# Zero rows of a padded weight by DMA, and up to two repeats of a score pass, in a fused attention and MLP kernel

## The chip, the cores and the metric

The kernel runs on one core of one Trainium2 chip. The metric is the device time of one execution in microseconds (us); lower is better. A kernel's time is the median of several executions. A profile is one further execution, recorded by the hardware profiler: its span is the time from the first to the last instruction.

## The reference

The sequence has S = 2048 rows of D = 640 bf16 values; attention has H = 32 heads of Dh = 20; the MLP has 1536 hidden columns. All of it is computed from one input x:

```python
g = sigmoid((x * gate_w).sum(-1, keepdims=True))
q, k, v = split(x @ wqkv)                    # 32 heads of 20
a = softmax(q @ k.T * Dh**-0.5) @ v          # per head, over all 2048 keys
a = concat_heads(a) @ wo
h = x @ w1 + b1
b = (h * tanh(softplus(h))) @ w2
out = g * a + (1 - g) * b
```

## The kernel before

**Units and slots.** Heads are taken in NG = 8 groups of HG = 4, queries in NC = 4 chunks of 512, keys in 16 tiles of 128. One unit is (c, g, kt, j): the scores of 512 queries of chunk c against 128 keys, for head j of group g. There are 2048 units, packed three to a slot, so 683 slots. A slot fills three PSUM banks, and there are two such sets of banks (banks 0 to 2 and 3 to 5). TensorE writes the three score tiles of a slot as one pass (L778: three matmuls of 32 rows that stand in different rows of the array). ScalarE takes the exponential of all three banks in one instruction (L806, 128x1536) and writes bf16 to one of five ETS buffers. TensorE multiplies these with v (L903, four heads at a time, in bank ACC = 6). Column 0 of v is one, so the sums of the softmax come out as a row of the same product.

**Units on VectorE.** In some slots the third unit is computed on VectorE instead, by bit arithmetic and a polynomial: L820 reads the bank, then L838, L840, three L843 and one L844 give the exponential in an OFF buffer. The exponential on ScalarE is then 128x1024. `choose` decides this from how far VectorE is behind in the plan.

**Background work.** Bank FB = 7 is shared by all else that TensorE does: projections to Q and K (L447, evicted by VectorE at L464) and V (L479, L487), the MLP's first product (L595, L605), its second (L659, evicted at L666), and the product with wo (L683, evicted and mixed at L689). Only one task holds the bank at a time, and the next must wait for the eviction. The mish function of the MLP is on ScalarE (L625) and VectorE (L645 to L652).

**The plan.** The order of instructions on every engine is written out ahead of time by a Python planner. `pl.now[engine]` is the planner's own clock of each engine, and each operation has a fixed cost. Per step the planner emits the exponential of slot `step` (`emit_e`), the scores of slot `step + 2` (`emit_s`), perhaps a repeat of that score pass (`repeat_s`, L790), the start of a VectorE unit (`emit_x`), at most two passes of products with v (`emit_pv`), and background matmuls. Engines run their instructions strictly in this order. So a matmul that waits holds all later matmuls.

A repeat writes the same scores into the same banks again. It is put where TensorE's planned stream of work would otherwise be less than STREAM = 0.46 of ScalarE's planned time; `to_come` counts the products and background work that the same step is expected to add. The exponential waits for the last repeat.

**End of a group of heads.** When the 16 key tiles of a (c, g) are through, `emit_off` must first have brought in all units of that group that VectorE computes; until then `emit_pv` returns without a product ("stuck"). Then VectorE copies bank ACC to OUNG (L967), SP sends the four rows of sums to RR (L970), VectorE inverts them (L974), SP writes them to SUMS in DRAM (L975) and spreads them to BCT (L977), and VectorE multiplies (L946) into OTN, or into QT for chunks 2 and 3.

**The padded output weight.** A head's 21 rows (sum and 20 values) stand at partitions 32j to 32j + 20, so wo is laid out in WOQ with the same gaps: rows 32j + 1 to 32j + 20 hold wo, the other 48 rows must be zero. WOQ holds the padded query weights first. When the last Q projection is issued, `load_wo` puts one memset of all of WOQ (128x5120) on GpSimd (L578) and four DMAs of wo on SP (L581), which wait for the memset. GpSimd also copies the padded weights of Q and K (L436).

Of the kernel before, what the change touches and what calls it, by code (L numbers as in the profile page):

```python
# [9 lines left out]
BF16 = mybir.dt.bfloat16  # L10
# [6 lines left out]
P = 128  # L17
S = 2048
D = 640
NF = 1536  # L20
H = 32
DH = 20
NG = 8
HG = 4
# [21 lines left out]
HOP = 0.1  # L46
TAIL = {"pe": 0.17, "act": 0.12, "dve": 0.125, "pool": 0.1, "sp": 2.0}
SWITCH = 0.1
COL = 1 / 2400.0
PASS = CW * COL  # L50
EXP = 1.335
STREAM = 0.46
EXP_PAIR = 0.908
# [124 lines left out]
def bass_gated_mix__softmax_full_mha__dense_activation_mish__prompt_kernel(  # L178
# [30 lines left out]
    WOQ = sb("WOQ", [P, NG * D], BF16)  # L209
# [4 lines left out]
    OTN = sb("OTN", [P, 2, NG, CW], BF16)  # L214
# [18 lines left out]
    FLAG = sb("FLAG", [1, 1], I32)  # L233

    SUMS = nc.dram_tensor("SUMS", [HG, CW], FP32, kind="Internal")

    def xt(c):
        return XB[:, c, :].rearrange("p (f t) -> p f t", t=CW)
# [38 lines left out]
    WOG = WOQ[:, :].rearrange("p (g c) -> p g c", c=D)  # L277
# [11 lines left out]
    off = {}  # L289
    off_units = {}  # L290

    def attention(pl, fast):
# [7 lines left out]
        soon = [deque() for _ in range(LANES)]  # L300
        norm = deque()
        acts = deque()
        now = {"step": -1, "open": None, "bank": False, "rate": 9.0}


        if fast:
# [7 lines left out]
        low_last = [None]  # L314
# [62 lines left out]
        wkv_read, wq_read = [], []  # L377
# [5 lines left out]
        wog_ready = []  # L383
# [5 lines left out]
        if fast:  # L389
# [17 lines left out]
            m_padq = pl.add("dve", lambda e: e.memset(PADQ, 0.0), cost=0.4)  # L407
            m_padk = pl.add("dve", lambda e: e.memset(PADK, 0.0), cost=0.4)
            m_acc = pl.add("dve", lambda e: e.memset(PS[:, ACC, :], 1.0), cost=0.5)
            m_one = pl.add("pool", lambda e: e.memset(V_all[:, :, :, 0:1], 1.0), cost=2.4)  # L410

            warm = None
            for i in range(20):
# [8 lines left out]
                B1T[:, :], B_b1.rearrange("(f p) -> p f", p=P), allow_slow_non_contiguous=True), (), "b1")  # L422
            g_load = pl.add("pool", lambda e: e.dma_start(
                GW[:, :], gate_w.rearrange("(f p) -> p f", p=P), allow_slow_non_contiguous=True), (), "gw")
            gw_col = pl.add("pool", lambda e: e.tensor_copy(WV[:, :, D], GW[:, :]), [g_load])
            pad_done, pad_read = {}, {}

# [147 lines left out]

            def load_wo():
                assert len(sq_ops) >= 4
                z = pl.add("pool", lambda e: e.memset(WOQ[:, :], 0.0), list(wq_read), cost=4.7)  # L578
                wo_v = A_wo.rearrange("(g j r) c -> j r g c", g=NG, j=HG, r=DH)
                for j in range(HG):  # L580
                    wog_ready.append(pl.add("sp", lambda e, j=j: e.dma_start(  # L581
                        WOG[32 * j + 1:32 * j + 1 + DH, :, :], wo_v[j]), [z], f"wo{j}", cost=0.6))

            h_done, b_read = {}, {}
            u_free, w_free = [None, None], [None]
# [116 lines left out]
        def p_task(c, t, half, due):  # L702

            tb = c * 4 + t

            def ready():
                if any((c, g) not in otn_done for g in every) or (fast and (tb, half) not in bdone):
                    return None
                if fast and len(wog_ready) < HG:
                    return None  # L710
                return [otn_done[(c, g)] for g in every] + wog_ready

            def finish(bank, last):
                otn_read[c % 2].append(last)
                ev = mix(OUTT[:, of(half)], bank, tb, ball(tb)[:, of(half)],
                         [last, bdone.get((tb, half)), *out_dma.values()])
                if half == 1:
                    store(tb, OUTT[:, :], [ev])
                return ev

            return Task([p_mm(c, t, half, g, every) for g in every], HALF * COL, finish, due, ready)
# [36 lines left out]
        queue = deque()  # L758
        hold = {"until": 0}
# [27 lines left out]
        def repeat_s(s):  # L787

            for i, (c, g, kt, j) in enumerate(slots[s]):
                s_op[s] = pl.add("pe", lambda e, i=i, c=c, g=g, kt=kt, j=j: e.matmul(  # L790
                    scores(s)[:, i, :], KT[32 * j:32 * j + 32, g, kt * P:(kt + 1) * P],
                    QT[32 * j:32 * j + 32, g, c * CW:(c + 1) * CW], start=True, stop=True,
                    tile_position=(32 * j, 0)), [], cost=PASS if i == 0 else 0.004, kind="S")
# [113 lines left out]

        def emit_pv(step, passes):

            while passes and step >= hold["until"]:  # L910
                if not queue:
                    return
                c, g, kt, _ = queue[0][2]
                emit_off((c, g), False)
                n = HG - sum(u[2] == kt for u in off_units.get((c, g), ()) if fast)
                if len(queue) < n:
                    return
                if kt == NKT - 1 and not emit_off((c, g), True):
                    if step < NSLOT - 1:
                        return  # L920
                    flush(lambda: emit_off((c, g), True, True))
                passes -= 1
                for k in range(n):
                    s, i, (c, g, kt, j) = queue.popleft()
                    op = pv_slot[s] = pv(c, g, kt, j, ETS[:, s % NETS, i, :], [e_op[s]], k == 0)
                    pv_left[s] -= 1
                if kt == NKT - 1:
                    hold["until"] = step + PV_HOLD
                    group_done(c, g, step, op)
# [4 lines left out]
        def group_done(c, g, step, last):  # L934


            end = c == NC - 1 and g == NG - 1

            def reads():
                if fast:  # L940
                    return [low_last[0]] if c >= 2 else []
                assert c < 2 or g > 0 or len(otn_read[c % 2]) == 8
                return otn_read[c % 2]

            def times(src, deps):
                oung_free[0] = bc_read[0] = otn_done[(c, g)] = pl.add("dve", lambda e: e.tensor_tensor(  # L946
                    otn(c, g, fast), src, BC, ALU.mult), [*deps, *reads()], cost=WIDE)
                if g == NG - 1:
                    otn_read[c % 2] = []

            if end:
                while norm:
                    norm.popleft()[1]()
                flush(lambda: not any(soon))
                src = PS[:, ACC, :]
                a = pl.add("dve", lambda e: e.transpose(BC, src), [last, bc_read[0]], cost=0.7)
                a = pl.add("dve", lambda e: e.reciprocal(RR[:, :], BC[:, 0:CW:32]), [a, rr_read[0]], cost=0.25)
                a = pl.add("dve", lambda e: e.transpose(
                    BC.rearrange("p (a r) -> p a r", r=32), RR[:, :].unsqueeze(2).to_broadcast([P, 16, 32])),
                    [a], cost=0.7)  # L960
                times(src, [a])
                acc_free[0] = oung_free[0]
                return
            while oung_free[0] == "busy":
                norm.popleft()[1]()
            src = OUNG[:, :]
            ev = dve(lambda e: e.tensor_copy(src, PS[:, ACC, :]), [last, oung_free[0]], WIDE)  # L967
            oung_free[0] = "busy"
            acc_free[0] = ev
            got = pl.add("sp", lambda e: e.dma_start(  # L970
                RR[:, :], OUNG[0:P:32, :].rearrange("j (r a) -> j r a", a=16)), [ev, rr_read[0]], "nr0", cost=0.55, tail=1.4)

            def invert():
                r = pl.add("dve", lambda e: e.reciprocal(RR[:, :], RR[:, :]), [got], cost=0.25)  # L974
                rr_read[0] = pl.add("sp", lambda e: e.dma_start(  # L975
                    SUMS.ap().rearrange("j (r a) -> (j r) a", a=16), RR[:, :]), [r, *spread_last], "nr1", cost=0.4, tail=1.7)
                spread_last[:] = [pl.add("sp", lambda e: e.dma_start(  # L977
                    BC, SUMS.ap().unsqueeze(1).to_broadcast([HG, 32, CW])),
                    [rr_read[0], bc_read[0]], "nr2", cost=0.55, tail=4.7)]
                spread = list(spread_last)  # L980
                norm.append((WIDE, lambda: times(src, spread), lambda: spread[-1]))
            norm.append((0.25, invert, lambda: got))
# [126 lines left out]
        for step in range(NSLOT + 40):  # L1109
# [28 lines left out]
            if step + 2 < NSLOT:  # L1138
                compose(step + 2, choose(step + 2) if fast and (step < slot_of(0, 1, 0) or behind < CATCH_UP) else None)
                emit_s(step + 2)  # L1140

                to_come = 0.0 if step < hold["until"] else min(2, len(queue) // HG) * PASS
                if owed + rate > 0.1 and pick(pl.now["pe"] + 0.8):
                    to_come += min(owed + rate, 0.4)
                if share[-1][0] + PASS + to_come < STREAM * (share[-1][2] + (EXP_PAIR if fast and step + 1 in off else EXP)):
                    repeat_s(step + 2)
                if fast and step + 2 in off:
                    emit_x(step + 2)
            emit_pv(step, 2 if step < NSLOT - 1 else 99)
# [15 lines left out]
        c = NC - 1  # L1165
# [151 lines left out]
```

## Time and profile before

| | |
|---|---|
| Three runs | 924.34, 927.46, 927.84 us (median 927.46) |
| Profiled execution | 926.2 us, of which the span is 924.3 us |
| TensorE clock granted, mean | 0.982 of full speed |
| Busy: ScalarE, VectorE, TensorE (matmul) | 895.4, 840.5, 771.0 us |
| GpSimd | 18.5 us in 25 instructions |
| Exponentials L806 | 683, of them 122 two banks wide |
| VectorE units (L820) | 58 + 63 = 121 |
| Score matmuls L778, repeated ones L790 | 2048, 465 |

How to read the lines below: PE is TensorE (PEld its weight loads), ACT ScalarE, DVE VectorE, POOL GpSimd, SP the engine that issues most DMAs. A line of the timeline has the start and the length in us, the engine, the source line, the operation with output and input tiles, the count, and in brackets how long the engine had stood idle and what released it. The page cuts the span into 40 slices of 23.1 us; its digits are tenths.

### The profile page before, as it was taken

The numbers are of one execution on the slowest core, as the hardware profiler recorded it, in microseconds if no ns is written. First come the engines' busy times: TensorE is split into PE (matmuls) and PEld (weight loads), VectorE is DVE, ScalarE is ACT, GpSimd is POOL, SyncE is SP. The second block draws the span as 40 slices with busy tenths as digits, with TensorE's granted clock in tenths as the row PEclk, the third lists the DMA queues.
The fourth block names the chain that finished last, engine by engine and source line by source line (L and its number), as shares of the span: only waits on it lengthen the run. The fifth ranks groups of instructions, "written<-read, shape, count | busy, mean of one in ns | idle before, by whom it ended". The sixth has DMA issues, their size and how long they took to land.

```text
span 924.3 us, 16089 instructions
## 1 busy us (share of the span) xinstructions
PE 771.0 (83%) x6649; PEld 262.2 (28%) x6701; DVE 840.5 (91%) x1561; ACT 895.4 (97%) x738; POOL 18.5 (2%) x25
## 2 busy tenths in 40 slices
PE   7788888887888888787998888889878888887986
PEld 2223222222323323232233222223223332232232
DVE  2498998789999999998999999999999999999874
ACT  5999999999999999998999999999999999999995
POOL 1000000000000000001000000000000000000000
PEclk9999999999999999998999999999999999999598
DMA  9001000000010100004111111111111211110001
GB/s 221 1 14 41 13 14 13 2 27 27 28 41 28 29 27 28 13 14 139 24 39 38 56 54 39 51 38 49 48 38 41 62 48 42 48 51 14 13 13 33
DMA packets 63136, 35.97 MB, mean 39 GB/s; under 512 B 22224, under 2 KB 59088, under 8 KB 63056
## 3 DMA queue, kind: packets, MB, share of 16 engines
q1 hardware_dynamic: 59040, 32.40, 13.1%
q10 hardware_dynamic: 3936, 2.46, 0.9%
q8 instruction: 55, 0.90, 0.4%
q14 instruction: 25, 0.20, 0.1%
q0 software_dynamic: 80, 0.00, 0.0%
HBM read 29.10 MB, written 2.88 MB: 35 GB/s over the span
## 4 chain that ended last, share of the span: by engine, by line
ACT 91%; PE 4%; DVE 3%; DMA 1%; issue 0%
ACT ETS L806 89%; PE PS L778 1%; ACT U L625 1%; ACT REG L625 1%; DMA XB<-in_A_x_dram 1%; PE PS L903 1%; PE PS L659 1%; DVE OFF L840 1%; PE PS L447 0%; PE PS L790 0%; ACT W2R L625 0%; DVE W2R L843 0%; DVE ETS L689 0%; DVE REG L820 0%; PE PS L479 0%
## 5 line engine op out<-in xcount | busy, mean ns | idle before, releaser
L806 ACT ACTIVATE ETS<-PS 128x1536 bf16<-128x1536 f32 (+1 forms) x683 | 884.2, 1578 | 8.9 <-PE PS L778 7.2
L778 PE MATMUL PS<-QT,KT 32*128 32x512 bf16 x2048 | 272.9, 390 | 127.0 <-ACT ETS L806 115.9
L903 PE MATMUL PS<-ETS,V_all 128*21 128x512 bf16 x1927 | 212.3, 391 | 0.2
L778 PEld LDWEIGHTS PS<-QT,KT 32*128 32x128 bf16 x2048 | 67.2, 91 | 350.0 <-ACT ETS L806 330.5
L648 DVE RECIPROCAL T<-T 128x256 f32<-128x256 f32 x48 | 83.4, 1738 | 0.0
L903 PEld LDWEIGHTS PS<-ETS,V_all 128*21 128x21 bf16 x1927 | 48.5, 89 | 119.7 <-issue 111.1
L659 PE MATMUL PS<-W2R,HB 128*128 128x320 bf16 x384 | 73.6, 311 | 4.1 <-DVE QT L464 3.4
L790 PE MATMUL PS<-QT,KT 32*128 32x512 bf16 x465 | 62.7, 391 | 0.0
L595 PE MATMUL PS<-XB,REG 128*128 128x256 bf16 x360 | 53.2, 275 | 0.0
L820 DVE TENSOR_SCALAR W2R<-PS 128x512 int32<-128x512 f32 x58 | 39.4, 686 | 13.1 <-PE PS L778 12.0
L820 DVE TENSOR_SCALAR REG<-PS 128x512 int32<-128x512 f32 x63 | 42.9, 682 | 5.4 <-PE PS L778 2.9
L447 PE MATMUL PS<-XB,WOQ 128*128 128x512 bf16 x135 | 40.2, 383 | 5.9 <-issue 2.4
L447 PE MATMUL PS<-XB,REG 128*128 128x512 bf16 x133 | 40.9, 384 | 3.9 <-issue 2.4
L843 DVE SCALAR_TENSOR_TENSOR REG<-REG,EM 128x512 f32<-128x512 f32 x64 | 43.5, 679 | 0.1
L844 DVE SCALAR_TENSOR_TENSOR OFF<-REG,OFF 128x512 bf16<-128x512 f32 x63 | 42.8, 681 | 0.1
L843 DVE SCALAR_TENSOR_TENSOR REG<-REG,ER 128x512 f32<-128x512 f32 x62 | 42.0, 678 | 0.2
L659 PEld LDWEIGHTS PS<-W2R,HB 128*128 128x128 bf16 x384 | 30.5, 99 | 39.9 <-issue 24.9
L843 DVE SCALAR_TENSOR_TENSOR W2R<-W2R,EM 128x512 f32<-128x512 f32 x58 | 39.5, 681 | 0.2
L843 DVE SCALAR_TENSOR_TENSOR W2R<-W2R,ER 128x512 f32<-128x512 f32 x58 | 39.4, 679 | 0.1
L844 DVE SCALAR_TENSOR_TENSOR OFF<-W2R,OFF 128x512 bf16<-128x512 f32 x58 | 39.0, 678 | 0.2
L595 PEld LDWEIGHTS PS<-XB,REG 128*128 128x128 bf16 x360 | 29.3, 98 | 22.1 <-issue 19.7
L479 PE MATMUL PS<-REG,XB 128*128 128x80 bf16 (+1 forms) x640 | 33.0, 201 | 2.1 <-DVE MXS L544 1.5
(101 smaller groups left out, 813.4 us busy)
## 6 DMA issues: line engine op xcount, KB each, us to landing
REG<-in_B_w_dram SPq DMA_DIRECT2D x36, 320.0 KB, 3.2
BCT<-SUMS SPq DMA_DIRECT2D x31, 256.0 KB
W2R<-in_B_w_dram SPq DMA_DIRECT2D x12, 320.0 KB, 3.2
W2R<-in_B_w_dram SPq DMA_DIRECT2D x1, 1920.0 KB, 8.0
out_dram<-OUTT SPq DMA_DIRECT2D x12, 160.0 KB, 1.8
REG<-in_A_wqkv_dram ACTq DMA_DIRECT2D x2, 700.0 KB, 5.9
WOQ<-in_A_wo_dram SPq DMA_DIRECT2D x4, 200.0 KB
WOQ<-in_A_wqkv_dram ACTq DMA_DIRECT2D x1, 700.0 KB, 8.6
```

Of the source, the lines that this page charges most:

```text
L447: return lambda e, bank: e.matmul(PS[:, bank, :], pads[:, b, f, :], xt(c)[:, f, :], start=(f == 0), stop=(f == NFT - 1))
L479: return lambda e, bank: e.matmul(PS[:, bank, t * n:(t + 1) * n], xt(c)[:, f, t * P:(t + 1) * P], WV[:, f, g * HD:g * HD + n], start=(f == ...
L595: return lambda e, bank: e.matmul(PS[:, bank, i * HW:(i + 1) * HW], w1b(n1)[:, f, i * P:(i + 1) * P], xt(c)[:, f, cols], start=(f == 0), s ...
L648: piece(RECIP, lambda e: e.reciprocal(T1[:, :], T1[:, :]))
L659: return lambda e, bank: e.matmul(PS[:, bank, 0:HALF], HB[:, hc % 2, f, t * P:(t + 1) * P], W2[:, f, half * HALF:(half + 1) * HALF], start ...
L778: last = pl.add("pe", lambda e, i=i, c=c, g=g, kt=kt, j=j: e.matmul(scores(s)[:, i, :], KT[32 * j:32 * j + 32, g, kt * P:(kt + 1) * P], QT ...
L790: s_op[s] = pl.add("pe", lambda e, i=i, c=c, g=g, kt=kt, j=j: e.matmul(scores(s)[:, i, :], KT[32 * j:32 * j + 32, g, kt * P:(kt + 1) * P], ...
L806: e_op[s] = pl.add("act", lambda e: e.activation(ETS[:, s % NETS, 0:n, :], scores(s)[:, 0:n, :], AF.Exp, scale=SCALE), [s_op[s], pv_slot.g ...
L820: ev_op[s] = dve(lambda e: e.tensor_scalar(x, scores(s)[:, 2, :], SCALE * LOG2E, BIAS, ALU.mult, ALU.add), [s_op[s], ei_free[b], *(wkv_rea ...
L843: piece(WIDE, lambda e, i=i: e.scalar_tensor_tensor(r, r if i else m, POLY[i], m, ALU.add, ALU.mult))
L844: piece(WIDE, lambda e: e.scalar_tensor_tensor(to, r, POLY[3], to, ALU.add, ALU.mult))
L903: return pl.add("pe", lambda e: e.matmul(PS[32 * j:32 * j + EW, ACC, :], V_all[:, kt, h, :], src, start=(count == 0), stop=(count == NKT - ...
```

## The change

1. `load_wo` no longer puts a memset on GpSimd. The four wo DMAs wait directly for the readers of the old contents. Five more DMAs on SP write the zero rows: one for partitions 0, 32, 64 and 96, and one for each of the four gaps of eleven rows. Their source is a new DRAM row ZEROS, read once for each destination row.
2. ZEROS is filled at the start: VectorE zeroes a corner of OTN (8 x 640), and a DMA on GpSimd's queue, put ahead of the copy `gw_col`, sends it to DRAM. The first products into OTN depend on that DMA.
3. A product with WOQ is ready when any entry is in `wog_ready` (there are now nine, all put in at once), and depends on all of them.
4. `emit_pv` records in `now["stuck"]` that products were held up by VectorE units. The next step then counts no products in `to_come`.
5. Up to two repeats of a score pass per step instead of one. The second must fit under the same target with its own length added. Each repeat must also end, by the planner's clock, before the running exponential does.

```diff
+    ZEROS = nc.dram_tensor("ZEROS", [1, NG * D], BF16, kind="Internal")
...
+            blank = OTN[0:NG, 0, 0:2, :].rearrange("p g t -> p (g t)")[:, 0:D]
+            m_blank = pl.add("dve", lambda e: e.memset(blank, 0.0), cost=0.25)
...
+            zeros = pl.add("pool", lambda e: e.dma_start(
+                ZEROS.ap().rearrange("o (g c) -> (o g) c", c=D), blank), [m_blank], "zero")
             gw_col = pl.add("pool", lambda e: e.tensor_copy(WV[:, :, D], GW[:, :]), [g_load])
...
             def load_wo():
-                z = pl.add("pool", lambda e: e.memset(WOQ[:, :], 0.0), list(wq_read), cost=4.7)
                 wo_v = A_wo.rearrange("(g j r) c -> j r g c", g=NG, j=HG, r=DH)
                 for j in range(HG):
                     wog_ready.append(pl.add("sp", lambda e, j=j: e.dma_start(
-                        WOG[32 * j + 1:32 * j + 1 + DH, :, :], wo_v[j]), [z], f"wo{j}", cost=0.6))
+                        WOG[32 * j + 1:32 * j + 1 + DH, :, :], wo_v[j]), list(wq_read), f"wo{j}", cost=0.6))
+                for n, rows in enumerate([slice(0, P, 32)] + [slice(32 * j + 1 + DH, 32 * j + 32) for j in range(HG)]):
+                    dst = WOQ[rows, :]
+                    wog_ready.append(pl.add("sp", lambda e, dst=dst: e.dma_start(
+                        dst, ZEROS.ap().to_broadcast([dst.shape[0], NG * D])), [*wq_read, zeros], f"wz{n}", cost=0.6))
...
-                if fast and len(wog_ready) < HG:
+                if fast and not wog_ready:
                     return None
...
         def emit_pv(step, passes):
+            now["stuck"] = False
...
                     if step < NSLOT - 1:
+                        now["stuck"] = True
                         return
...
-                    return [low_last[0]] if c >= 2 else []
+                    return [low_last[0]] if c >= 2 else [zeros]
...
-                to_come = 0.0 if step < hold["until"] else min(2, len(queue) // HG) * PASS
+                to_come = 0.0 if step < hold["until"] or now["stuck"] else min(2, len(queue) // HG) * PASS
...
-                if share[-1][0] + PASS + to_come < STREAM * (share[-1][2] + (EXP_PAIR if fast and step + 1 in off else EXP)):
-                    repeat_s(step + 2)
+                next_exp = EXP_PAIR if fast and step + 1 in off else EXP
+                want = STREAM * (share[-1][2] + next_exp)
+                for n in range(1, 3):
+                    if (share[-1][0] + n * PASS + to_come < want
+                            and pl.now["pe"] + PASS + TAIL["pe"] + 2 * HOP <= pl.now["act"] + next_exp):
+                        repeat_s(step + 2)
```

More of the change, by code (lines that the diff above doesn't have):

```diff
@@ L302, in attention @@
         acts = deque()
-        now = {"step": -1, "open": None, "bank": False, "rate": 9.0}
+        now = {"step": -1, "open": None, "bank": False, "rate": 9.0, "stuck": False}
         if fast:
```

## The prediction

> **What bounds the kernel now.** I read the page first (busy shares, then the slices), then the stretches view around the slices where ScalarE or the TensorE clock dips, then the timeline there, the chain of waits for the pace, and the view of waits.
>
> ```profile
> PE 771.0 (83%) x6649; PEld 262.2 (28%) x6701; DVE 840.5 (91%) x1561; ACT 895.4 (97%) x738; POOL 18.5 (2%) x25
> ...
> ACT  5999999999999999998999999999999999999995
> ...
> PEclk9999999999999999998999999999999999999598
> ...
> ACT ETS L806 89%; PE PS L778 1%; ACT U L625 1%; ACT REG L625 1%; DMA XB<-in_A_x_dram 1%; PE PS L903 1%; PE PS L659 1%; DVE OFF L840 1%; PE PS L447 0%; PE PS L790 0%; ACT W2R L625 0%; DVE W2R L843 0%; DVE ETS L689 0%; DVE REG L820 0%; PE PS L479 0%
> ```
>
> ScalarE is the bound: 97% busy, and its exponentials (L806) are 89% of the chain. So a change can only gain where ScalarE idles or is given less work. ScalarE has one dip inside the span (19th slice), and the clock has two (19th and 38th).
>
> ```profile
> 429.00:442.00 13.00, 9.10 (x56) 2.54 (x55) 11.69 (x17) 8.35 (x7) 4.36 (x1) 0.74 0.33 66
> 853.00:876.00 23.00, 22.36 (x142) 4.42 (x138) 19.30 (x35) 21.48 (x17) 0.00 (x0) 0.55 0.05 14
> 442.00:853.00 411.00, 349.53 (x2979) 123.39 (x2975) 406.71 (x743) 411.00 (x346) 0.00 (x0) 1.00 0.15 43
> ```
>
> In these stretches (columns: length, then busy time of PE, PEld, DVE, ACT, POOL, then clock and DMA) ScalarE is without a gap from 442 to 853, loses 4.65 us in the first dip and 1.52 us in the second. The first dip, in the timeline:
>
> ```profile
> 429.75 4.36 POOL L578 MEMSET WOQ<- 128x5120 bf16 x1 [96.46 <-PE PS L447]
> 430.19 4.21 DVE L840 TENSOR_SCALAR OFF<-REG 128x512 uint16<-128x512 uint16 x1
> 434.14 1.52 SPq L581 DMA_DIRECT2D WOQ<-in_A_wo_dram  x4
> 434.31 0.67 DVE L464 CAST QT<-PS 128x512 bf16<-128x512 f32 x1
> 435.13 1.23 PE L659 MATMUL PS<-W2R,HB 128*128 128x320 bf16 x4 [3.35 <-DVE QT L464]
> 436.95 1.45 ACT L806 ACTIVATE ETS<-PS 128x1536 bf16<-128x1536 f32 x1 [3.25 <-PE PS L778]
> 439.20 1.45 ACT L806 ACTIVATE ETS<-PS 128x1536 bf16<-128x1536 f32 x1 [0.80 <-PE PS L778]
> ```
>
> An L840 that elsewhere takes 0.42 us took 4.21 us, and ended just after the GpSimd memset did. Behind it on VectorE stood the eviction L464 of bank FB; TensorE, in order, stood 3.35 us at the matmul L659 that needs that bank, with the next scores behind it; ScalarE ran dry for 3.25 us. TensorE then had half its clock (0.50 in the stretches from 435 to 440), which gave the 0.80 and, at 441.25, another 0.59.
>
> **Part 1, the memset goes.** The pace of ScalarE comes from the chain: six wide exponentials in a row took 8.06 us, so 1.343 each; a run of six with one two-bank exponential took 7.63, so 0.915 for that one. In the dip the run before ended at 433.70, of which 0.11 is the tail of a lone one (1.45 against 1.343), and two wide ones lie between there and 441.25: 441.25 - 433.59 - 2 x 1.343 = 4.97 us lost. Without the memset L840 takes 0.42, L464 starts near 430.6 and TensorE does not stop; next late is nothing before ScalarE itself. Gain 5.0; bounds 3.25 (if the clock falls anyway) to 5.0.
>
> **Part 2, the zeros by DMA.** The memset of 8 x 640 on VectorE: 0.59 us at most (the row of L407, 128 x 640), in the 2.52 us for which VectorE waits for its first weights. The DMA that fills ZEROS on GpSimd's queue: 0.87 to 1.17 us (rows of L421, L423) inside GpSimd's 6.19 us wait for GW. The first OTN product waits for ZEROS too; it runs at 55.3 us and the nearest DMAs there took 7.0 us: nothing. On SP four loads of wo now issue at about 430.25 instead of 434.14, and five zero DMAs behind them: 1.52 + 5 x 0.38 = 3.4 us, so SP is free at 433.7; the next on SP, SUMS<-RR, went at 436.98. Their 480 KB take 2.0 us at the rate of W2R (1920 KB in 8.0) or 3.7 at the rate of wo here (130 GB/s); WOQ is first read by L683 at 489.9. Behind them in the queue stand SUMS and BCT of one normalisation; before, SUMS took 5.6 us to land behind the wo loads and VectorE waited for a BCT only once, 0.6 us. The test for readiness (any load in wog_ready, not four) and the nine loads that a product with WOQ names instead of four have one answer: all landed long before 489.9. Price 0, bounds 0 to 3.7. Without the 50 us of cover it would be the whole 3.7.
>
> **Part 3, repeats.** Scores are repeated (L790, 465 matmuls, 155 passes) to keep TensorE busy. Three edits: the planner drops a repeat that by its own clock would end after the running exponential; it allows a second one; and it no longer credits products that are stuck.
>
> The first edit. Three-bank repeats under a two-bank exponential have almost no room: 0.915 + 1.343 us until the exponential that needs them, less 1.45 (release of the bank), 0.15 (hand-off), 0.39 (scores) and 0.22 (repeat) leaves 0.05. About 15 of the 155 lie there in the timeline. Gain at most 15 x 0.22 = 3.3; at least 0; I take 1.0, since the page puts few waits of ScalarE to L790 (1.4 us, 4 times, most of it in the two dips).
>
> The second edit, cold stretch at 853 to 876. From 850.54 to 874.79 the timeline has 6 + 1 + 10 exponentials, three of them two-bank (evictions L820 at 857.63, 861.59, 865.68): 24.25 - 14 x 1.343 - 3 x 0.915 = 2.70 us lost. The clock falls at 854 after a step with scores, one repeat and no products (850.51 to 852.35), where a second repeat would fit. Gain 0 to 2.7; I take half, 1.35, for the drop may come elsewhere. Price of a second repeat at full clock: 2 x 1.343 - 1.45 - 0.15 - 0.39 - 2 x 0.22 leaves 0.26 us: nothing. It also takes room from other TensorE work, and all that the planner orders after a new repeat shifts: every short stall outside the dips is drawn anew (the largest, at 190.64, is 1.59 us), and so is the number of slots with a third bank on VectorE (121; one more or fewer is 1.343 - 0.915 = 0.43 us). Nothing gives this a sign; I take a loss of 0.5, with 3 either way.
>
> Sum: -5.0 - 1.35 - 1.0 + 0.5 = -6.85 us. The profiled execution took 926.2 (span 924.3 and 1.9 around it), 1.3 below the median of the three runs and inside their spread; its own time would become 919.3, and I count from the median: 927.46 - 6.85 = 920.6.
>
> **Rivals.** (a) *The stalls come back elsewhere.* The new order has its own in-order waits. For: VectorE is 99% busy from 442 to 853, so any late eviction there stops TensorE as L464 did. Against: in those 411 us ScalarE had no gap at all. If it gives back 3 to 6 of the 6.85 the time is 923.5 to 927; I put 925.
>
> (b) *Second repeats at half clock, slower.* The planner does not know the clock. At half clock a score pass shows 0.61 us and each repeat adds 0.43, so two repeats need 0.15 + 0.61 + 0.86 = 1.62 where 2 x 1.343 - 1.45 = 1.24 is there: ScalarE loses 0.38 us in each of the 15 or so wide steps of such a 20 us stretch, 5.8 us more than the 2.7 now. One such stretch: 927.46 - 5.0 - 1.0 + 0.5 + 5.8 = 927.8, level; two, the second with its own 2.7 as well: 936.3. It decides from the second stretch on. Against: repeats are there to end such a stretch. The half clock held from 854.0 to 874.4 though TensorE was marked busy for 22.36 of 23.00 us, so busy time alone did not lift it; it rose three microseconds after L659 came. The Trainium skill (TensorE: Matmul & The Clock Gate, "What's actually happening") has the clock return after one busy window of about 3.4 us; by that rule the loss would be two or three steps, about 1 us a stretch, and the sum would stand at 921 even with one. This trace does not agree: about six such lengths passed.
>
> (c) *The zeros or the guard change nothing.* If the 4.21 us were not the memset's doing, part 1 is 0 and the time 925.6; the ends of the two instructions, 434.11 and 434.40, speak against.
>
> **Numbers.** Forecast 0.62, (a) 0.22, (c) 0.05, (b) 0.11. A measurement here can tell about 0.5%, 4.6 us, from no change: faster means under 922.8. The forecast's own range, 915 to 925, loses some 0.05 above 922.8, and (a) with its lucky end gives 0.04 back: faster 0.61. Slower means above 932.1: only (b) from the second stretch and an unlucky new order, 0.10. Same: the rest, 0.29. The range: low, all gains whole (5.0 + 2.7 + 3.3) and a lucky order, 915; high, (b) with one stretch, 928.5.
>
> **What would show it.** Right: no L578; L840 at 0.42 us there; no clock dip and ScalarE without a gap near 430; wo and zero loads on SP before 434; L790 not under two-bank exponentials; the second dip shorter or gone. Wrong: new stalls of several microseconds of ScalarE behind L778 at other places, half-clock stretches with six L790 a step, or far fewer than 121 L820.

## The result, and the profile after

| | before | after |
|---|---|---|
| median (16 runs each) | 926.59 us | 930.59 us |
| lowest and highest | 924.34, 929.09 | 926.22, 932.87 |
| profiled execution: span | 924.3 | 928.3 |
| last exponential starts | 912.0 | 913.1 |
| from there to the end | 12.3 | 15.2 |
| repeated score matmuls | 465 | 510 |

The ratio is 1.0036, 95% interval 1.0022 to 1.0050: slower by 4.0 us, inside the half per cent that the prediction called no change, and above the top of its range (928.5). The median of the runs and the profiled span grew by the same 4.0 us, so the profile can be read for the cause. The source lines have moved by up to 14: the exponential is now L814, the scores L786, the repeat L798, the products with v L911, the OTN product L956, the wo loads L585, the zero loads L589, the product with wo L691 and its eviction L697.

The page of the profile after, in the places shown of before:

```profile
PE 779.0 (84%) x6695; PEld 267.2 (29%) x6746; DVE 839.4 (90%) x1569; ACT 894.8 (96%) x738; POOL 14.9 (2%) x25
...
ACT  5999999999999999999899999999999999999994
...
PEclk9999999999999999999899999999999999998698
...
ACT ETS L814 87%; PE PS L786 1%; ACT U L633 1%; DMA SUMS<-RR 1%; ACT REG L633 1%; DMA XB<-in_A_x_dram 1%; PE PS L911 1%; PE PS L798 1%; DMA BCT<-SUMS 1%; PE PS L452 0%; DVE REG L851 0%; PE PS L667 0%; PE PS L691 0%; PE PS L603 0%; ACT W2R L633 0%; DVE ETS L697 0%
```

GpSimd's busy time fell by 3.6 us, so the memset is gone. ScalarE does the same work and still has one dip, but a slice later (the 20th, not the 19th). Two transfers that the list of before did not name have joined it: SUMS<-RR and BCT<-SUMS, the two DMAs of a normalisation. The stretches view of after (length, busy PE, PEld, DVE, ACT, POOL, clock, DMA share, GB/s):

```profile
415.80:438.90 23.10, 19.52 (x167) 6.39 (x168) 18.82 (x38) 23.10 (x21) 0.00 (x0) 1.00 0.60 161
438.90:462.00 23.10, 19.34 (x139) 5.93 (x139) 17.97 (x35) 18.60 (x16) 0.00 (x0) 0.85 0.11 22
853.00:881.00 28.00, 24.48 (x175) 5.21 (x172) 25.20 (x46) 25.66 (x20) 0.00 (x0) 0.63 0.03 11
```

ScalarE has no gap in the 19th slice, where it had lost 3.75 us. In the 20th it lost 4.50 us, and the clock fell with it to 0.85. In the stretch at half clock near the end it loses 2.34 us of 28 where it had lost 1.58. The timeline of after around the new dip:

```profile
430.11 1.71 SPq L585 DMA_DIRECT2D WOQ<-in_A_wo_dram  x4
430.93 0.41 DVE L848 TENSOR_SCALAR OFF<-REG 128x512 uint16<-128x512 uint16 x1
431.85 2.21 SPq L589 DMA_DIRECT2D WOQ<-ZEROS  x5
434.11 0.35 SPq L985 DMA_DIRECT2D SUMS<-RR  x1
443.52 0.54 SPq L987 DMA_DIRECT2D BCT<-SUMS  x1
448.55 0.69 DVE L956 TENSOR_TENSOR OTN<-OUNG,BCT 128x512 bf16<-128x512 f32 x1 [4.55 <-DMA BCT<-SUMS]
450.24 0.39 PE L911 MATMUL PS<-OFF,V_all 128*21 128x512 bf16 x1 [1.70 <-DVE OFF L852]
451.48 1.02 ACT L814 ACTIVATE ETS<-PS 128x1024 bf16<-128x1024 f32 x1 [1.45 <-PE PS L786]
```

and the chain of waits in the same window, which ties the first half of it together (start, length, what):

```profile
434.11 9.39 DMA SUMS<-RR
443.50 0.02 issue
443.52 5.01 DMA BCT<-SUMS
448.53 0.02 issue
448.55 0.69 DVE OTN L956
```

Read from the top: the step that took 4.21 us takes 0.41 (L848), as forecast, and the loads go out 3.9 us earlier, as forecast. But 8 KB of sums, issued on SP behind 1280 KB of loads, took 9.39 us to land. BCT could be issued only then, and took 5.01 more. VectorE, in order, stood 4.55 us at the OTN product. Behind it stood the VectorE unit whose OFF the product L911 needs; TensorE stood there for 1.70 us with the next scores behind it; ScalarE ran dry, and half a clock until 457.5 made the next two exponentials late as well. In a steady run the next exponential starts 1.330 us after a wide one and 0.904 us after a two-bank one. (The prediction's 1.343 and 0.915 come from merged rows with their tail in them, so its 4.97 us are 5.1.) Against that pace three exponentials came 1.59, 2.36 and 0.93 us late: 4.9 us. In the kernel before, three were late in the old dip: 3.49, 0.92 and 0.71, together 5.1. The stall was not removed but moved by 15 us.

The other place is the end. The timeline of after, behind the last exponential (913.1):

```profile
917.12 0.69 DVE L956 TENSOR_TENSOR QT<-PS,BCT 128x512 bf16<-128x512 f32 x1
917.73 0.54 DVE L697 SCALAR_TENSOR_TENSOR W2R<-PS,GATE,XB 128x320 f32<-128x320 f32 x1
918.33 3.98 PE L691 MATMUL PS<-WOQ,QT 128*128 128x320 bf16 x16 [1.85 <-DVE W2R L697]
921.48 0.53 ACT L1197 ACTIVATE EM<-PS,GATE 128x320 f32<-128x320 f32 x1 [7.08 <-PE PS L691]
```

and of before, where the last exponential started at 912.0:

```profile
913.70 1.12 PE L683 MATMUL PS<-WOQ,QT 128*128 128x320 bf16 x7
915.55 0.69 DVE L946 TENSOR_TENSOR QT<-PS,BCT 128x512 bf16<-128x512 f32 x1
916.30 1.40 PE L683 MATMUL PS<-WOQ,QT 128*128 128x320 bf16 x9 [1.48 <-DVE QT L946]
917.06 0.53 ACT L1183 ACTIVATE EM<-PS,GATE 128x320 f32<-128x320 f32 x1 [3.77 <-PE PS L683]
```

Before, seven of the sixteen closing products with wo ran while VectorE normalised the last group. After, the plan had one partial product more (six matmuls) behind the last product with v. Its eviction from bank FB (L697, at 917.73) stood on VectorE behind the normalisation, and the sixteen closing products start with bank FB, so none ran before 918.33: ScalarE waited 7.08 us there, not 3.77, and the end took 2.9 us longer.

Late starts against that pace are called stalls from here on, and those of over 0.06 us are counted one by one. The 4.0 us of the span, then: the dip is level (5.2 us lost from 430 to 460 in both); the end is +2.9; all else up to the last exponential is +1.5 (stalls of over 0.06 us outside the dip +0.4, smaller ones +1.3, the first exponential 0.2 earlier); one more two-bank exponential gives back 0.4. One profile each is a thin base for the +0.4: a kernel below (e4) with after's plan up to the closing products lost 1.4 us more up to 430 than after did (8.3 against 6.9).

### The profile page after: what moved, and what is told of

Same layout as the page of the kernel before. It is cut to its first block, busy times and chain, and to the rows that moved or that the text cites. A ratio compares the mean times of both kernels' runs of the same rounds, so it can differ in the third digit from the quotient of the medians.

```text
span 928.3 us, 16199 instructions
## 1 busy us (share of the span) xinstructions
PE 779.0 (84%) x6695; PEld 267.2 (29%) x6746; DVE 839.4 (90%) x1569; ACT 894.8 (96%) x738; POOL 14.9 (2%) x25
## 3 DMA queue, kind: packets, MB, share of 16 engines
q1 hardware_dynamic: 59136, 32.89, 13.1%
## 4 chain that ended last, share of the span: by engine, by line
ACT 90%; PE 5%; DVE 3%; DMA 2%; issue 0%; ACTq 0%
ACT ETS L814 87%; PE PS L786 1%; ACT U L633 1%; DMA SUMS<-RR 1%; ACT REG L633 1%; DMA XB<-in_A_x_dram 1%; PE PS L911 1%; PE PS L798 1%; DMA BCT<-SUMS 1%; PE PS L452 0%; DVE REG L851 0%; PE PS L667 0%; PE PS L691 0%; PE PS L603 0%; ACT W2R L633 0%; DVE ETS L697 0%
## 5 line engine op out<-in xcount | busy, mean ns | idle before, releaser
L814 ACT ACTIVATE ETS<-PS 128x1536 bf16<-128x1536 f32 (+1 forms) x683 | 884.6, 1595 | 10.8 <-PE PS L786 7.9
L786 PE MATMUL PS<-QT,KT 32*128 32x512 bf16 x2048 | 274.2, 390 | 126.9 <-ACT ETS L814 114.5
L911 PE MATMUL PS<-ETS,V_all 128*21 128x512 bf16 x1926 | 212.7, 392 | 0.2 <-ACT ETS L814 0.2
L786 PEld LDWEIGHTS PS<-QT,KT 32*128 32x128 bf16 x2048 | 66.9, 91 | 348.2 <-ACT ETS L814 327.3
L911 PEld LDWEIGHTS PS<-ETS,V_all 128*21 128x21 bf16 x1926 | 48.2, 89 | 114.7 <-issue 107.1
L798 PE MATMUL PS<-QT,KT 32*128 32x512 bf16 x510 | 59.8, 393 | 0.0
L613 DVE TENSOR_TENSOR HB<-PS,B1F 128x512 bf16<-128x512 f32 x48 | 32.6, 679 | 1.5 <-PE PS L603 1.4
```

The costliest lines, as they stand in the source:

```text
L613: ev = dve(lambda e: e.tensor_tensor(hb, PS[:, bank, :].rearrange("p (i t) -> p i t", i=2), bias, ALU.add), [last, *b1f, *sq_read.values() ...
L786: last = pl.add("pe", lambda e, i=i, c=c, g=g, kt=kt, j=j: e.matmul(scores(s)[:, i, :], KT[32 * j:32 * j + 32, g, kt * P:(kt + 1) * P], QT ...
L814: e_op[s] = pl.add("act", lambda e: e.activation(ETS[:, s % NETS, 0:n, :], scores(s)[:, 0:n, :], AF.Exp, scale=SCALE), [s_op[s], pv_slot.g ...
L911: return pl.add("pe", lambda e: e.matmul(PS[32 * j:32 * j + EW, ACC, :], V_all[:, kt, h, :], src, start=(count == 0), stop=(count == NKT - ...
```

## The experiments

All ratios are to the kernel before, run on the same chip in the same batch (its medians there 926.63, 926.60, 927.05 and 926.46 us). Each kernel has its own line numbers.

**My theory** was: the early loads hold up the sums in SP's queue, which costs what the memset had cost; the rest is the new order of work, at the end above all; the repeats bring nothing. **The rivals**: the repeats themselves cost the time; or the order alone does, and the loads are a bystander.

**One part alone: the zeros without the new repeats (e1).**

```diff
-  to_come = 0.0 if step < hold["until"] or now["stuck"] else ...
+  to_come = 0.0 if step < hold["until"] else ...
-  for n in range(1, 3): ...            (the new rule)
+  if share[-1][0] + PASS + to_come < STREAM * (...): repeat_s(step + 2)
```

> The changed kernel with its zero rows by DMA, but with the repeats of before (one at most, old condition, no stuck flag). Theory A (the loss is in the zero DMAs: the sums of one normalisation land 9.4 us after their issue behind 1.28 MB of weight loads, VectorE stands 4.55 us at the product with BCT, ScalarE loses about 4.9 us): the wait for BCT is there again (2 to 5 us) and the time is near the kernel before, 925 to 930. Rival B (the loss is in the second repeats at half clock): the time falls to 921 to 923, since the memset stall is gone and nothing took its place.

928.08 us, ratio 1.0007 (0.9993 to 1.0021). The sums took 9.1 us here too (issued 434.23, BCT 443.33) and the view of waits has the same row:

```profile
DVE OTN L956 <- DMA BCT<-SUMS: 4.1, 1, 4.1
```

So the zero rows alone give nothing, and for the reason seen in after. The first exponential starts at 13.6 us (13.7 in before), and the stalls up to 430 come to 6.5 us in both, so the start-up part of the edit costs nothing, as priced.

**The other part alone: the new repeats with the memset (e2).**

```diff
(before, with now["stuck"] and the new rule for repeats; load_wo unchanged)
```

> The kernel before, memset kept, with only the new rule for repeats. Theory A: the memset stall of about 5 us is there as before; the new rule alone is within 2 us of before, or up to 3 us slower if the last 22 products with wo stand behind one late eviction at the end as in the changed kernel (2.9 us there). Rival B: 4 us or more slower than before, from half-clock stretches with six repeated matmuls a step.

933.22 us, ratio 1.0064 (1.0043 to 1.0086). The time is the one that rival B asked for. The memset's stall is there as in before (5.2 us), the end takes 15.4 us after the last exponential, much as in after, and 543 matmuls are repeated. No gain is to be seen anywhere; whether the rule or its order costs the rest is taken up below.

**Only the zeros later on SP (e3).**

```diff
+  def zero_rows():
       for n, rows in enumerate([...]): ... (the five zero DMAs)
+  later(now["step"] + 14, zero_rows)
-  if fast and not wog_ready:
+  if fast and len(wog_ready) < 2 * HG + 1:
```

> The changed kernel, only that the five zero DMAs are put on SP 14 steps (about 19 us) later, behind the sums of that normalisation; products with wo are ready only when all nine loads are put in. Theory A: the sums land in some 5 us instead of 9.4, VectorE's wait for BCT falls from 4.55 us to under 1, no half clock near 452, and the median falls by 3 to 5 us against the changed kernel, to 926 or 927. Rival B: the dip near 452 goes but the time stays within 1 us of 930.6, as the loss is in the repeats.

933.43 us, ratio 1.0067 (1.0039 to 1.0095): a miss. The timeline shows why the stall stayed:

```profile
434.33 0.36 SPq L988 DMA_DIRECT2D SUMS<-RR  x1
440.25 0.54 SPq L990 DMA_DIRECT2D BCT<-SUMS  x1
440.83 2.18 SPq L591 DMA_DIRECT2D WOQ<-ZEROS  x5
448.63 0.69 DVE L959 TENSOR_TENSOR OTN<-OUNG,BCT 128x512 bf16<-128x512 f32 x1 [5.60 <-DMA BCT<-SUMS]
452.22 2.91 ACT L817 ACTIVATE ETS<-PS 128x1536 bf16<-128x1536 f32 x2 [5.97 <-PE PS L789]
```

The sums now took 5.9 us, behind the four wo loads alone, against 9.4 behind nine: that half holds. But SP ran ahead of the plan. With nothing to wait for, the zero DMAs went out 0.04 us after BCT, and BCT, in flight beside them, took 8.4 us and not 5.0. A place later in the plan is not a later time: only a wait is. The dip, 7.2 us here, explains 2.0 of the 4.4 us by which this profile's span (932.7) exceeds after's; the rest is stalls elsewhere.

**All nine loads behind the product that they had held up (e5).**

```diff
+  q_all.append(True)
+  later(now["step"] + 14, load_rows)
+  def load_rows():
+      after = [*wq_read, bc_read[0]]       (bc_read[0]: the last reader of BCT)
       ... the nine DMAs, depending on after
-  if not gate_done or not w2_load or not wog_ready:
+  if not gate_done or not w2_load or not q_all:
```

> The changed kernel, only that all nine loads into WOQ wait for the product with BCT of that normalisation (L946 of the kernel before), so that no weight load is in the DMA queue beside its sums. Theory A (weight and zero loads delay SUMS and BCT; in the run before this one the zero loads were issued 0.6 us after BCT and took it from 5.0 to 8.4 us): VectorE's wait for BCT falls from 4.55 us to under 0.5, no half clock at 446 to 457, ScalarE without a gap of over 1 us there; median 4 to 6 us under the changed kernel, 925 to 927. Rival B (the loss is all in the repeats): the dip goes, the time stays above 929.

927.35 us, ratio 0.9999 (0.9985 to 1.0014): 3.2 us below after, with the same repeats, where 4 to 6 were expected. The profiled execution took 924.22, below that median. The timeline:

```profile
433.91 0.33 SPq L992 DMA_DIRECT2D SUMS<-RR  x1
435.34 0.54 SPq L994 DMA_DIRECT2D BCT<-SUMS  x1
442.54 0.68 DVE L963 TENSOR_TENSOR OTN<-OUNG,BCT 128x512 bf16<-128x512 f32 x1
443.25 1.52 SPq L592 DMA_DIRECT2D WOQ<-in_A_wo_dram  x4
444.81 2.21 SPq L596 DMA_DIRECT2D WOQ<-ZEROS  x5
```

With no loads ahead of them the same sums took 1.43 us, the OTN product did not wait, and the stretches view has ScalarE busy for 23.10 of 23.10 us in both slices, at a clock of 1.00. From 430 to 460 ScalarE lost 0.3 us where after lost 5.2. This settles the new stall: it is the loads. It does not bring the kernel below before.

**The end: the closing products start with other banks (e4).**

```diff
-  [FB, 0, 1, 2, 3, 4, 5, ACC], ...
+  [0, 1, 2, 3, 4, 5, FB, ACC], ...
```

> The changed kernel, only that in the closing products with wo bank FB comes seventh of eight and not first. Theory A's second part (after the last exponential, 16 products wait for the eviction of bank FB, which stands behind four steps of the last normalisation on VectorE, and then run at half clock: 2.9 us): TensorE does the first half of those products during that normalisation, ScalarE's wait at the end falls from 7.1 to about 4 us, the time by 2 to 3 us, to about 928. Rival: the end is set by the last normalisation alone and the time stays within 0.5 us.

928.93 us, ratio 1.0014 (0.9995 to 1.0032), 1.7 us below after, with intervals that overlap. Six of the sixteen closing products ran beside the normalisation where none had, ScalarE's wait there fell from 7.1 to 4.8 us, and the end took 12.9 us.

**Controls: the kernel before with a number of the planner moved a little,** VectorE's risk 0.50 to 0.52 (e6), and patience 12.0 to 12.3 (e7). Neither has a meaning for the change; both make the planner write another order.

> A control: the kernel before, with nothing of the change, only the planner's margin for late VectorE results 0.52 us instead of 0.50. The same work in a newly drawn order. Theory C (a new order alone moves the time by a few us, by its short stalls and by how many closing products wait for the last eviction; here 16 as before): within 2 us of before. If it is 4 us or more away, the losses of 3 to 6 us from the repeats cannot be told from a new draw.

> A second control: the kernel before, only the planner's patience for the steps of mish 12.3 us instead of 12.0. A new order in which 29 products with wo follow the last product with v, 16 in the kernel before, 22 in the changed one. Theory C: 2 to 5 us slower than before, most of it after the last exponential. Rival: the same time, as the end is set by the last normalisation.

925.86 us (0.9992, 0.9980 to 1.0004) and 934.75 us (1.0090, 1.0073 to 1.0107). The second was expected 2 to 5 us slower and is 8 us slower. In it, 29 products with wo stood behind the last product with v (16 in before), and bank FB had to be emptied three times behind the normalisation. Its timeline, from the last normalisation on:

```profile
918.64 0.69 DVE L946 TENSOR_TENSOR QT<-PS,BCT 128x512 bf16<-128x512 f32 x1
919.85 0.99 PE L683 MATMUL PS<-WOQ,QT 128*128 128x320 bf16 x6 [2.80 <-DVE W2R L689]
921.49 1.78 PE L683 MATMUL PS<-WOQ,QT 128*128 128x320 bf16 x6 [0.65 <-DVE W2R L689]
923.91 4.21 PE L683 MATMUL PS<-WOQ,QT 128*128 128x320 bf16 x16 [0.65 <-DVE W2R L689]
```

The end took 18.8 us against 12.3, so 6.5 of the 9.5 us by which the profiled span grew (to 933.8) lie behind the last exponential. A new order alone can cost twice what the whole change did.

**Variants of the repeats on the kernel before.** Up to two without the guard, and the guard with one repeat:

```diff
 (before, memset kept)
+  for n in range(1, 3):                    # e8: two, no guard
+      if share[-1][0] + n * PASS + to_come < want: repeat_s(step + 2)
 (before, memset kept)
+  for n in range(1, 2):                    # e12: one, with the guard
+      if (share[-1][0] + n * PASS + to_come < want
+              and pl.now["pe"] + PASS + TAIL["pe"] + 2 * HOP <= pl.now["act"] + next_exp): ...
```

> The kernel before, memset kept, up to two repeats by the old condition, without the rule that a repeat must end before the running exponential and without the stuck flag (597 repeated matmuls, 465 before, 543 with the whole new rule). Theory B (second repeats lengthen what stands ahead of the products when the clock is half: in the run with the repeats alone, six repeats at half clock from 348.08 took 1.07 us and ScalarE then waited 0.73 and 1.83 us for L903): as slow as the repeats alone or slower, 931 to 936, with short half-clock stretches of 3.4 us each costing 1 us or more. Rival: the rule on the end of the exponential is what costs, and this is within 2 us of before.

> The kernel before, memset kept, one repeat at most, and dropped when by the planner's clock it ends after the running exponential (411 repeated matmuls for 465). 22 closing products behind the last eviction, not 16. Theory: the first edit of the repeats is worth -1 us, the longer end +1.5 to 3: 927 to 929. Rival: fewer repeats leave TensorE at half clock more often and it is 4 us or more slower.

933.83 us (1.0082, 1.0065 to 1.0099) and 932.63 us (1.0062, 1.0034 to 1.0090). In the first, 597 matmuls are repeated, and between 800 and 850 us, where before lost 0.4 us, ScalarE lost 6.3, with 13.7 us at half clock there. In the second the guard, taken alone, did not bring the microsecond that was expected: its stalls of over 0.06 us are 19.4 us in sum where before had 18.0, and the end took 15.0.

**Both repairs together, with the new repeats and with the old, and with the guard alone.**

```diff
 (after, with the late loads and the closing order above)   # e9
 (the same, old rule for repeats)                           # e10
 (the same, old rule with the guard, one repeat)            # e11
```

> The changed kernel with both repairs: all nine loads behind the normalisation, and bank FB seventh in the closing products. New repeats kept. Theory A (the two costs are separate and add): 927.35 less the 1.7 us that the order of the banks gave alone, 925 to 926, 0.1 to 0.2% under before. Rival: one repair takes back what the other gave, and the time stays at 927.

> As the run with both repairs, but with the repeats of before (one at most; 429 repeated matmuls for 510). Theory B (the new repeats cost time at half clock): 1 to 4 us under the run with both repairs, 922 to 924.5. Theory A alone (the new repeats cost nothing by themselves): within 1 us of the run with both repairs. The memset is gone in both.

> As the run before it in this list, but a repeat is also dropped when by the planner's clock it ends after the running exponential (387 repeated matmuls). If the short waits of ScalarE behind repeats under two-bank exponentials cost 1 us, as the prediction had it, 0.5 to 1.5 us faster; if the clock needs those repeats, slower, with more half-clock stretches.

924.26 us (0.9971, 0.9958 to 0.9984), 922.62 us (0.9954, 0.9937 to 0.9971) and 924.01 us (0.9970, 0.9956 to 0.9985). All three are faster than before and after. The 4.4 us of e10 (927.05 - 922.62) look like the memset's 5 us, but they hold for this one order: the same kernel in two other orders (e13 and e14, below) takes 931.00 and 928.00 us. The new rule and the guard each lost about 1.5 us against e10, but the controls say that such a difference may be the order's.

**Rule or order.** Two more pairs, old rule and new rule, on the base with both repairs, each pair at one of the two neutral numbers.

```diff
 (e10 and e9, each with "dve": 0.52 in RISK)     # e13 old rule, e15 new rule
 (e10 and e9, each with PATIENCE = 12.3)         # e14 old rule, e16 new rule
```

> The late loads and the other closing order with the old repeat rule (922.62 us before), its order drawn anew by a number of the planner (VectorE's risk 0.50 to 0.52) that is neutral in meaning. Both theories take it as the base of a pair with the new repeat rule at the same number. If a new order is only a draw, it lies anywhere from 921 to 931; if the order before was nothing special, within 1.5 us of 922.6.

> As the run before, drawn anew by another number (patience 12.0 to 12.3), which on the kernel before cost 8 us, seven of them after the last exponential with 29 closing products. The closing order here no longer starts behind bank FB, so at most half of that should come back: 922 to 927 us.

> The same as the first of these four (risk 0.52) with the new repeat rule. Theory A, the rule costs time by itself (second repeats in cold stretches, products that stand behind repeats): slower than its partner by 1 to 3 us, as 924.26 against 922.62. Theory B, the rule costs nothing and only draws another order: the difference to its partner has no sign, anywhere from -4 to +4 us.

> The same as the second of these four (patience 12.3) with the new repeat rule. Theory A: slower than its partner by 1 to 3 us, so that all three pairs have one sign. Theory B: no sign; one of the two new pairs at least comes out level or faster.

| pair (old rule, new rule) | median us | last exponential starts | from there to the end | products with wo behind the last with v |
|---|---|---|---|---|
| e10, e9 | 922.62, 924.26 | 908.4, 909.9 | 12.7, 13.2 | 22, 22 |
| e13, e15 | 931.00, 925.87 | 911.2, 910.3 | 17.9, 14.7 | 34, 28 |
| e14, e16 | 928.00, 921.33 | 907.6, 908.6 | 19.2, 13.1 | 29, 22 |

The ratios to before of e13 to e16, in this order: 1.0045 (1.0031 to 1.0058), 1.0016 (1.0004 to 1.0028), 0.9995 (0.9986 to 1.0004) and 0.9940 (0.9924 to 0.9955). The pairs differ by +1.6, -5.1 and -6.7 us: not one sign, as theory A asked, and twice beyond the 4 us that theory B allowed. So the draw decides, and it decides at the end: of -5.1 and -6.7 us, the profiles have -3.2 and -6.1 behind the last exponential. Up to it the new rule differs by +1.5, -0.9 and +1.0 us: never the 2.35 of gain that was forecast. The closing order with bank FB late did not protect e14 as expected: there it is partial products, planned one after another through bank FB, that wait for the normalisation, and ScalarE stood 10.8 us at the end.

One cost does go with the rule. Stalls of at most 0.06 us add up to 1.9 to 2.2 us in each of the eight kernels with the new rule (2.2 in after), and to 0.9 to 1.4 us in each of the ten without it (0.9 in before). So about 1 us belongs to the rule in every order. Neither the guard alone (e11 and e12: 1.1 and 1.3) nor two repeats without it (e8: 1.4) shows it, and what makes these exponentials late was not followed up.

e16 (late loads, closing order, new rule, patience 12.3) is the fastest kernel of the study: 921.33 us, 5.1 below before in the same batch. That this is close to the forecast of 920.6 is luck: the same source with two other numbers in the planner takes 924.26 and 925.87 us.

## Why the prediction was wrong

**Right.** The memset's stall and its 4.97 us: L848 took 0.41 us, TensorE did not stop, and with the loads out of the way the gain was there (0.3 us lost from 430 to 460 in e5 and e10, 5.2 in before). The start-up cost of nothing (e1). The loads at 430.1 and SP free by 434. Rival (a), that the stalls come back elsewhere, is what happened, though it named no place and put the time at 925; its chance of 0.22 was too low. Its evidence against (no gap of ScalarE from 442 to 853) concerned the old order only, and was misread: the record of a wide exponential is about 1.6 us long and the next one starts 1.330 us behind it, so a start that is 0.2 us late leaves no gap. From start to start, before lost 3.2 us between 442 and 853.

**The step that failed: part 2, priced at 0.** It asked when SP would be free (433.7) and when WOQ is first read (489.9), and it named the sums and BCT behind the loads, with the 5.6 us that the sums had taken behind four of them. Then it put the price to 0, because VectorE had hardly ever waited for a BCT. Much of that cover was the memset's own stall: in before the OTN product came at 450.49, 7.9 us after BCT was issued at 442.55, and part 1 took 5 us of this away. Rows of before would have shown it. There the sums landed 8.4 us after the first of the four loads was issued (434.14 to 442.55), so 800 KB went through at 95 KB per us, not at the 130 with which the prediction reckoned. At 95, 1280 KB take 13.5 us, from 430.1 to 443.6 (measured: 443.50). With the 5.0 us that BCT took in after this is 448.6 (measured: 448.55), and VectorE, 5.0 us earlier than in before, is at the product by 445.5: a wait of 3 us. The other 1.5 of the 4.55 us come from the new order: four short VectorE steps that stood ahead of the product in before stand behind it in after, where VectorE was free for it at 444.0. The upper bound that was given, 3.7 us, was too low too, as it had only the zeros in it and no price for the clock: measured, 4.9.

The Trainium skill (DMA: Bandwidth & Descriptors, Queues, rings and completion order) has SP's DMAs on one ring for each DMA engine, consumed in ring order. These traces agree for what stands behind: the same 8 KB took 1.4 us with nothing ahead of it (e5, e10), 5.6 to 5.9 behind 800 KB (before, e3), 9.1 to 9.4 behind 1280 KB (e1, after). Counted from the issue of the first load, the sums had landed after 8.4 and 8.6 us, and after 13.1 and 13.4 us: 94 to 98 KB per us in all four. The ring order does not give e3's other half: BCT, issued ahead of the zeros, still took 8.4 us instead of 5.0. Why is open; whether BCT's transfer shares its DMA engines or its memory with theirs was not measured.

**Part 3, -2.35 us, was mis-sized: about +1.** The guard does what it says: of 15 three-bank repeats under two-bank exponentials 2 are left. But e11 against e10 and e12 against before show no gain from it, though each is also a new order; that the 0.22 us lay beside work for which ScalarE did not wait is the likely reason, not a shown one. The second repeats did not keep the clock up: in after it fell at 853.4 and again at 870.5, 20.5 us in all as in before, and for 3.4 us each near 318 and 621, where before had no fall. With the small stalls that go with the rule, part 3 cost about 1 us. Where the clock is down, rival (b)'s price holds. Two lines of after's timeline at half clock:

```profile
857.09 1.06 PE L798 MATMUL PS<-QT,KT 32*128 32x512 bf16 x6
858.20 2.79 ACT L814 ACTIVATE ETS<-PS 128x1536 bf16<-128x1536 f32 x2 [0.22 <-PE PS L798]
```

Two exponentials every 3.02 us (855.18, 858.20, 861.21), where two wide ones at pace take 2.66: 0.36 us lost to each such step, priced 0.38. But it comes with every second exponential, not with every one, as (b) had it: the kernels with a stretch of 27.3 us and six repeats in it (e3, e4, e9, e16) lost 4.8 to 5.0 us from 850 to the last exponential, before lost 3.2, so 1.6 to 1.8 more where (b) priced 5.8.

The stretch view of one of them, e16:

```profile
849.50:876.80 27.30, 25.68 (x159) 4.98 (x159) 23.37 (x42) 24.04 (x19) 0.00 (x0) 0.50 0.03 11
```

TensorE is marked busy for 25.68 of 27.30 us and has half its clock throughout. The Trainium skill (TensorE: Matmul & The Clock Gate, What's actually happening) has the clock return after one busy window of about 3.4 us. Half-clock stretches here do last whole multiples of such a window (3.4, 6.8, 10.2, 20.5, 27.3 us), but marked busy time is not what lifts them: eight windows passed here, which bears out the prediction's doubt. What differs is the kind of work. The 18 profiles have 179 half-clock windows of 3.4 us between 14 and 900 us. The 80 behind which the clock rose hold on average 6 score matmuls (32 rows) and 11 others; the 99 behind which it stayed down hold 12 and 7. So repeats of scores fill TensorE's time but go with a clock that stays down; whether they are the reason was not tested.

**The new order, +0.5 with 3 either way, was mis-sized.** The sign was rightly left open, but the step left out the end: it counted short stalls of ScalarE and slots with two banks. After gave +2.9 at the end, +0.2 in stalls that do not go with the rule and -0.4 by the two-bank slot, 2.7 in all where 0.5 was taken; the first two controls alone lie 8.9 us apart. Of the 10.9 us between the forecast gain and the measured loss, then, some 5 are part 2, some 3.6 part 3 and some 2.2 the order. How many products with wo stand behind the last product with v (16 to 34), and which of them wait for bank FB, is drawn with each order, and it moved the end from 12.2 to 19.2 us.

## What to carry to other kernels

When a transfer is moved earlier, list what stands behind it in the same queue, add its bytes at the rate of that place, and follow the small transfers behind it to the instruction that needs them; do that with the times that the change gives, since the stall that it removes may have been their cover. A transfer that is to be late needs a wait for an event, as an engine that only issues can run ahead of the plan, as SP did in e3. Where a planner writes the order, a change to its inputs draws a new order: read the end of the kernel first, and run a control with a neutral number moved before a part of the change is credited or blamed with a few microseconds.

## What the runs showed of the hardware

A small transfer waits for the large ones ahead of it on its queue: 8 KB took 1.4, 5.6 to 5.9 and 9.1 to 9.4 us behind 0, 800 and 1280 KB, which went through at 94 to 98 KB per us. A transfer already issued was slowed as well: BCT took 8.4 us with 480 KB issued right behind it (e3), 5.0 with no load left in flight (after). TensorE kept half its clock for eight windows of 3.4 us in a row while it was marked busy for 94% of the time (25.68 of 27.30 us); what does lift the clock was not settled.
